# Warm-up matmuls at the head of a Fourier + soft-MoE kernel: six of 512 columns in one pass, or twelve of 64 columns in fp32

## The chip, the cores and the metric

The kernel runs on one core of a Trainium2 chip. A core has TensorE (in the profile PE for matmuls and PEld for weight loads), VectorE (DVE), ScalarE (ACT), GpSimd (POOL) and SyncE (SP, which here only issues DMAs); SPq is SP's instruction queue. The metric is the device time of one execution in microseconds. The profile comes from one further execution; its span runs from the first to the last instruction of the program.

## The reference

The input is `x` with 8 batches of 2496 tokens of 256 features. Each batch goes through a Fourier transform along the tokens, a complex linear layer, a soft threshold and the inverse transform; the result goes through a soft mixture of experts. Cut to what matters:

```python
X = np.fft.rfft(x, axis=1); Xr, Xi = X.real, X.imag
Yr = Xr @ w_r - Xi @ w_i + b_r
Yi = Xr @ w_i + Xi @ w_r + b_i
Yr = np.sign(Yr) * np.maximum(np.abs(Yr) - 0.01, 0.0)     # Yi likewise
y = np.fft.irfft(Yr + 1j * Yi, n=2496, axis=1)             # then, over all tokens:
logits = y @ phi
d = softmax(logits, over tokens); slot_input = d.T @ y      # 32 slots
slot_out = relu(slot_input @ w1[e]) @ w2[e]                 # per expert
out = softmax(logits, over slots) @ slot_out
```

## The kernel before

The transform of 2496 points is done in two stages, 39 x 64. Stage one multiplies the tokens with a table of 39-point Fourier factors (matmuls `pa`, and `q` for batch 0), stage two with 64-point factors (`px`), and the linear layer follows (`pk`, `py`). Later come the inverse stages, the slots, the experts and the output. Every engine runs its instructions in the order in which the code issues them; for most of the kernel a hand-made table of due times, `PLAN`, sets that order.

The head is what matters here. Before anything else GpSimd zeroes a tile `warm` of 128 x 128, and TensorE multiplies it with itself into a PSUM tile `wps` that nobody reads. These are the warm-up dummies:

```python
warm = wtile([128, 128], F32R, "k1", "warm")
P.memset(warm.bitcast(F32), 0.0)
wps = psum("ps", "wps")
for _ in range(6):
    mm(out=wps, lhsT=warm, rhs=warm.unsqueeze(1).broadcast_to([128, 4, 128]), start=True, stop=True)
```

`F32R` is fp32 in one pass: a matmul is one weight load and one pass of the moving columns. A matmul on plain `F32` operands stands in the trace as two weight loads and two passes. The broadcast makes 512 moving columns out of the 128 of `warm`.

Behind the dummies TensorE does batch 0's first stage as 44 plain fp32 matmuls `q` (a weight load of 128 columns of `x`, 120 moving columns of the Fourier table). They read the tile `xf`, which holds the table and the first tokens and comes by SyncE's first DMA, and ten more tiles of `x` that follow it. `wri`, the linear weights, comes behind those. While `q` runs, ScalarE and VectorE copy its results to `at` and `atr`; when `wri` is there, GpSimd makes `wsum` and a difference in place of `wri`, from which ScalarE and VectorE make the weights' high and low parts (`w_r`, `nws`, `wd`, each with `h` and `l`).

Then, in TensorE's order: transposes of `at` into `pa`, copied to `ap` by ScalarE; `px` of the first half of the features from that `ap`; the second half's transposes, copied to `ap` by VectorE; transposes for the next step; `px` of the second half. From each `px` ScalarE makes `xsm` and `xth`, VectorE `xsm` and the two halves of `xs`. `pk` reads `xs`, first for the first half of the features and then, behind six `py`, for the second.

Of the kernel before, what the change touches and what calls it, by code (L numbers as in the profile page):

```python
# [12 lines left out]
F32 = mybir.dt.float32  # L13
F32R = mybir.dt.float32r
# [174 lines left out]
def fourier_soft_moe_kernel(ctx: ExitStack, tc: tile.TileContext, t: dict, out: bass.AP):  # L189
# [21 lines left out]
    def psum(tag, name):  # L211
        return pp.tile([128, 512], F32, tag=tag, name=name, bufs=psum_bufs[tag])

    def wtile(shape, dt, tag, name):
        if tag == "rte":
            return wqp.tile(list(shape), dt, tag=tag, name=name, bufs=2)
        if tag in a_bufs:
            return wap.tile(list(shape), dt, tag=tag, name=name, bufs=a_bufs[tag])
        if tag in main_bufs:
            return wmp.tile(list(shape), dt, tag=tag, name=name, bufs=main_bufs[tag])  # L220
        return wcp.tile(list(shape), dt, tag=tag, name=name, bufs=chain_bufs[tag])
# [8 lines left out]
    V, A, P = (_InOrder(tc, e) for e in (nc.vector, nc.scalar, nc.gpsimd))  # L230
# [18 lines left out]
    def mm(**kw):  # L249
        tc.keep_in_program_order(nc.tensor.matmul(**kw))  # L250
# [39 lines left out]
        x0.append([xf[:P1, Q1 + e * D : Q1 + e * D + D] for e in range(GP)])  # L290
        pools["f1x"] = xf[:P1, :Q1].rearrange("p (c a r) -> p c a r", c=2, r=R)

    warm = wtile([128, 128], F32R, "k1", "warm")
    P.memset(warm.bitcast(F32), 0.0)
    wps = psum("ps", "wps")
    for _ in range(6):
        mm(out=wps, lhsT=warm, rhs=warm.unsqueeze(1).broadcast_to([128, 4, 128]), start=True, stop=True)

    while len(x0) < G // GP:
        load_x0()  # L300
# [907 lines left out]
    rhs = []  # L1208
# [98 lines left out]
    for j in range(NBLK):  # L1307
# [6 lines left out]
        if not pqs:  # L1314
            pqs = [(k, psum(("pf", "pl")[k % 2], f"pq{k}")) for k in ((0, 1) if j == 0 else (j,))]
            for a in range(2):
                for k, pq in pqs:
                    lo = k * TR - k * TR % F
                    mm(
                        out=pq,  # L1320
                        lhsT=cts[lo][:, k * TR - lo : k * TR - lo + TR],
                        rhs=rhs[a].rearrange("p b d -> p (b d)"),
                        start=(a == 0),
                        stop=(a == 1),
# [4 lines left out]
        if j + 1 == starts[i] + OUTS[i]:  # L1329
            n = OUTS[i] * 512  # L1330
            sp(
                out=out[128 * 512 * starts[i] : 128 * 512 * (j + 1)].rearrange("(p f) -> p f", p=128),
# [68 lines left out]
```

## Time and profile before

| | us |
|---|---|
| time, median of 3 runs | 517.67 |
| the three runs | 517.89, 517.67, 515.95 |
| time of the profiled execution | 516.78 |
| its span | 515.0 |
| busy in the span: TensorE passes, weight loads | 500.7, 440.1 |
| busy in the span: VectorE, ScalarE, GpSimd | 405.7, 312.6, 296.2 |

The time of the profiled execution is 1.78 us more than its span; that lies around the program's instructions. Passes overlap in the records, since the end of a pass is modelled and the next one starts before it.

### The profile page before, as it was taken

How to read it: one execution, taken by the hardware profiler on the slowest of the kernel's cores; microseconds unless marked ns; L12 is line 12 of the kernel's file. 1: busy time of each engine (PE TensorE's matmuls, PEld its weight loads, DVE VectorE, ACT ScalarE, POOL GpSimd, SP SyncE). 2: the span in 40 equal slices, each digit the busy share in tenths (PEclk: the TensorE clock that was granted, in tenths of full speed). 3: DMA queues.
4: the chain of work that ended last, by engine and by line, in shares of the span. 5: the costliest groups of instructions: out<-in, count | busy, mean ns of one | idle time of the engine just before them, and what ended most of it. 6: DMA issues, size and time to landing. Idle time of an engine off the chain costs nothing.

```text
span 515.0 us, 11951 instructions
## 1 busy us (share of the span) xinstructions
PE 500.7 (97%) x4475; PEld 440.1 (85%) x4475; DVE 405.7 (79%) x776; ACT 312.6 (61%) x704; POOL 296.2 (58%) x280
## 2 busy tenths in 40 slices
PE   8999999999999999999999999999999999999992
PEld 7889999999999999998999898889899878468881
DVE  2897787799968898889889988897898866257661
ACT  2776666777676766676667666655534446138761
POOL 0686786768676757675667577867475503153310
PEclk9999999999999999999999999999999999999997
DMA  8655555675665657565656566696685567959998
GB/s 299 229 186 185 182 171 201 177 242 149 257 181 183 165 194 203 175 167 201 188 174 174 211 186 207 163 307 182 242 256 150 199 163 194 410 198 403 408 419 342
DMA packets 87485, 114.91 MB, mean 223 GB/s; under 512 B 46191, under 2 KB 65119, under 8 KB 85891
## 3 DMA queue, kind: packets, MB, share of 16 engines
q1 hardware_dynamic: 86860, 113.65, 66.5%
q8 instruction: 35, 0.57, 0.5%
q10 hardware_dynamic: 567, 0.50, 0.3%
q14 instruction: 23, 0.19, 0.1%
HBM read 66.78 MB, written 47.34 MB: 222 GB/s over the span
## 4 chain that ended last, share of the span: by engine, by line
PE 84%; DMA 6%; DVE 4%; POOL 1%; ACT 1%; issue 1%; SPq 1%; DVEq 0%; ACTq 0%; POOLq 0%
PE py L250 21%; PE px L250 13%; PE pk L250 10%; PE pa L250 10%; PE pq L250 9%; PE pt L634 6%; PE pr L250 3%; PE pe L250 2%; PE pc L1186 2%; PE pL L250 2%; PE pg L250 2%; PE pd L250 1%; PE hps L250 1%; DMA out<-ost 1%; DMA gp<-gd 1%; DMA wri<-in_w 1%
## 5 line engine op out<-in xcount | busy, mean ns | idle before, releaser
L185 POOL TENSOR_TENSOR xs<-xsm,xs 128x256 fp32r<-128x256 f32 x77 | 63.3, 823 | 96.4 <-DVE xs L185 66.3
L185 POOL TENSOR_TENSOR rt<-ut,rt 128x512 f32<-128x512 f32 x79 | 104.7, 1326 | 15.1 <-DVE rt L185 13.8
L185 POOL TENSOR_TENSOR xl<-xr,xh 117x512 fp32r<-117x512 f32 x72 | 97.7, 1357 | 12.9 <-ACT xh L185 12.9
L250 PE MATMUL px<-smov,ap 128*128 128x128 f32 x640 | 85.1, 276 | 0.1
L250 PEld LDWEIGHTS px<-smov,ap 128*128 128x128 f32 x640 | 80.3, 192 | 4.8 <-DVE xsm L185 0.3
L185 DVE SCALAR_TENSOR_TENSOR ut<-py,pk,k 128x256 f32<-128x256 f32 x160 | 69.5, 475 | 11.7 <-PE py L250 11.0
L185 ACT CAST xth<-px 128x512 fp32r<-128x512 f32 x80 | 46.9, 587 | 43.6 <-PE px L250 21.6
L185 ACT COPY ast<-pa 128x512 f32<-128x512 f32 x75 | 44.2, 589 | 46.1 <-PE pa L250 46.1
L185 DVE TENSOR_TENSOR xtl<-px,xth 128x512 fp32r<-128x512 f32 x80 | 54.6, 683 | 18.6 <-ACT xsm L185 18.6
L250 PE MATMUL pk<-xs,w_rh 128*128 128x256 f32 (+1 forms) x320 | 66.1, 290 | 0.1
L185 DVE TENSOR_SCALAR rt<-ut 128x512 f32<-128x512 f32 x69 | 65.5, 949 | 0.6
L250 PE MATMUL py<-xth,nwsh 128*128 128x256 f32 (+1 forms) x160 | 53.2, 333 | 0.1
L250 PEld LDWEIGHTS pk<-xs,w_rh 128*128 128x128 f32 x320 | 51.9, 189 | 0.9 <-DVE xs L185 0.6
L185 ACT CAST xh<-xr 117x512 fp32r<-117x512 f32 x75 | 47.4, 635 | 0.4 <-DMA xr<-in_x 0.4
L634 PE MATMUL pt<-pk,rt 128*128 128x128 f32 x320 | 45.2, 274 | 0.0
L250 PE MATMUL py<-xth,wdh 128*128 128x256 f32 (+1 forms) x160 | 44.8, 280 | 0.0
L250 PE MATMUL py<-xtl,nwsh 128*128 128x256 f32 (+1 forms) x160 | 44.6, 279 | 0.0
L250 PE MATMUL py<-xtl,wdh 128*128 128x256 f32 (+1 forms) x160 | 44.5, 278 | 0.0
L250 PE MATMUL py<-xth,wdl 128*128 128x256 f32 (+1 forms) x160 | 44.5, 278 | 0.0
L250 PE MATMUL py<-xth,nwsl 128*128 128x256 f32 (+1 forms) x160 | 44.4, 278 | 0.0
L250 PE MATMUL pk<-xs,w_rl 128*128 128x256 f32 (+1 forms) x160 | 44.4, 278 | 0.0
L185 ACT COPY T<-pt 128x512 f32<-128x512 f32 x66 | 39.2, 601 | 6.8 <-PE pt L634 5.1
(197 smaller groups left out, 1192.3 us busy)
## 6 DMA issues: line engine op xcount, KB each, us to landing
xr<-in_x SPq DMA_DIRECT2D x35, 512.0 KB
ap<-adr SPq DMA_DIRECT2D x70, 256.0 KB
adr<-ast SPq DMA_DIRECT2D x21, 768.0 KB
out<-ost SPq DMA_DIRECT2D x12, 1024.0 KB
w<-in_moe_w SPq DMA_DIRECT2D x21, 512.0 KB
out<-ost SPq DMA_DIRECT2D x14, 512.0 KB
hl<-in_moe_w SPq DMA_DIRECT2D x6, 512.0 KB
x<-in_x SPq DMA_DIRECT2D x10, 256.0 KB
```

What stands on the lines that cost most here:

```text
L185: return lambda *a, **k: self.tc.keep_in_program_order(f(*a, **k))
L250: tc.keep_in_program_order(nc.tensor.matmul(**kw))
L634: tc.keep_in_program_order(nc.tensor.transpose(out=out, in_=in_, identity=identity))
L1186: nc.tensor.transpose(out=pc[:, i * P1 : (i + 1) * P1], in_=chls[b][x][:, 2 * (r + i) : 2 * (r + i) + 2].rearrange("p g h s -> p (g h s)") ...
```

## The change

The tile `warm` becomes plain fp32, and six dummies of 512 columns become twelve of 64. A plain fp32 matmul is two weight loads and two passes, so that 12 instructions of TensorE (6 and 6) become 48 (24 and 24).

```diff
-    warm = wtile([128, 128], F32R, "k1", "warm")
-    P.memset(warm.bitcast(F32), 0.0)
+    warm = wtile([128, 128], F32, "k1", "warm")
+    P.memset(warm, 0.0)
     wps = psum("ps", "wps")
-    for _ in range(6):
-        mm(out=wps, lhsT=warm, rhs=warm.unsqueeze(1).broadcast_to([128, 4, 128]), start=True, stop=True)
+    for _ in range(12):
+        mm(out=wps[:, :64], lhsT=warm, rhs=warm[:, :64], start=True, stop=True)
```

TensorE's instructions at the start of the program, before (a row is a run of equal matmuls; numbers at the end of a name are buffer numbers, and the weight loads are not listed):

```order
L1397 UNCONDITIONAL_BRANCH
L250 MATMUL wps<-warm 128x512 x6
L250 MATMUL q_0_150<-xf 128x2x20x3 x2
L250 MATMUL q_1_153<-xf 128x2x20x3 x2
L250 MATMUL q_0_150<-xf,x_2_89 128x2x20x3 x2
L250 MATMUL q_1_153<-xf,x_2_89 128x2x20x3 x2
```

and the same place of the changed kernel:

```order
L1397 UNCONDITIONAL_BRANCH
L250 MATMUL wps<-warm 128x64 x12
L250 MATMUL q_0_156<-xf 128x2x20x3 x2
L250 MATMUL q_1_159<-xf 128x2x20x3 x2
L250 MATMUL q_0_156<-xf,x_2_95 128x2x20x3 x2
L250 MATMUL q_1_159<-xf,x_2_95 128x2x20x3 x2
```

Only the row of the dummies differs: no other instruction of TensorE has moved against its neighbours, and on the other engines only buffer numbers differ.

## Rows read from the trace of the kernel before

**Rows 1.** The page: busy time by engine, then the chain's shares by engine
```profile
PE 500.7 (97%) x4475; PEld 440.1 (85%) x4475; DVE 405.7 (79%) x776; ACT 312.6 (61%) x704; POOL 296.2 (58%) x280
...
PE 84%; DMA 6%; DVE 4%; POOL 1%; ACT 1%; issue 1%; SPq 1%; DVEq 0%; ACTq 0%; POOLq 0%
```

**Rows 2.** Chain that ended last, first 30 us: start us, us, what
```profile
2.59 5.32 DMA x<-in_x
...
7.93 5.43 DMA wri<-in_w
...
14.84 1.62 POOL wri L185
...
20.00 0.68 PE py L250 x6
20.68 1.03 PE pk L250 x6
```

**Rows 3.** Timeline of TensorE's passes, 0 to 16 us: start, us, count, [idle before]
```profile
0.99 2.93 PE L250 MATMUL wps<-warm 128*128 128x512 f32 x6 [0.99 <-POOL warm L185]
4.46 1.15 PE L250 MATMUL q<-xf 117*128 117x120 f32 x8 [0.54 <-DMA xf<-in_xf]
```

**Rows 4.** Tile `wps`: durations in ns min/median/max, first and last start in us
```profile
L250 PEld LDWEIGHTS wps<-warm x6: 286/330/334, 1.0 to 2.9; 128*128 128x128 f32 x6
L250 PE MATMUL wps<-warm x6: 628/628/793, 1.0 to 3.3; 128*128 128x512 f32 x6
```

**Rows 5.** Groups by line and form, 24 to 40 us: busy us, mean ns
```profile
L250 PE MATMUL pa<-xl,f1h 117*128 117x512 f32 x7 | 2.8, 395 | 0.0
```

**Rows 6.** Groups of weight loads by line and form, 7.4 to 10 us
```profile
L250 PEld LDWEIGHTS q<-xf,x 117*128 117x128 f32 x25 | 2.9, 192 | 0.0
```

**Rows 7.** Timelines from 6.6 us: passes, then weight loads
```profile
6.63 7.41 PE L250 MATMUL q<-xf,x 117*128 117x120 f32 x64
...
6.63 7.22 PEld L250 LDWEIGHTS q<-xf,x 117*128 117x128 f32 x64 [0.31 <-DMA x<-in_x]
```

**Rows 8.** Timeline 13 to 20.5 us, all engines
```profile
15.20 1.11 PE L250 MATMUL px<-smov,ap 128*128 128x128 f32 x8
...
16.15 0.60 PE L634 MATMUL pa<-pk,at 128*128 128x128 f32 x4
16.16 0.83 DVE L185 SCALAR_TENSOR_TENSOR nwsl<-wsum,nwsh 128x512 fp32r<-128x512 f32 x1
...
16.48 0.62 ACT L185 CAST wdh<-wri 128x512 fp32r<-128x512 f32 x1 [0.35 <-POOL wri L185]
...
16.92 0.68 DVE L185 COPY ap<-pa 128x512 f32<-128x512 f32 x1
...
17.65 0.97 PEld L250 LDWEIGHTS px<-smov,ap 128*128 128x128 f32 x8 [0.27 <-DVE ap L185]
...
18.85 0.37 ACT L185 COPY xsm<-px 128x256 f32<-128x256 f32 x1 [0.79 <-PE px L250]
19.12 0.59 ACT L185 CAST xth<-px 128x512 fp32r<-128x512 f32 x1
...
19.76 0.41 DVE L185 TENSOR_TENSOR xsm<-px,xsm 128x256 f32<-128x256 f32 x1
...
20.20 0.29 DVE L185 CAST xs<-xsm 128x256 fp32r<-128x256 f32 x1
```

**Rows 9.** DMA queues: packets, MB, share of 16 engines' span
```profile
q8 instruction: 35, 0.57, 0.5%
```

**Rows 10.** Stretches: busy us (count) by engine, PEclk (granted clock), DMA share, GB/s
```profile
3.00:4.00 1.00, 0.92 (x3) 0.20 (x1) 0.00 (x0) 0.00 (x0) 0.00 (x0) 1.00 0.72 206
...
505.00:509.00 4.00, 0.00 (x0) 0.00 (x0) 0.76 (x2) 0.53 (x2) 0.00 (x0) 1.00 1.01 420
...
512.00:515.00 3.00, 0.00 (x0) 0.00 (x0) 0.00 (x0) 0.00 (x0) 0.00 (x0) 0.50 0.17 71
```

## The prediction

> **What bounds the kernel now.** I read the page first. TensorE's passes fill 97% of the span, and the chain of work that ended last lies on TensorE for 84% [rows 1]. So what delays TensorE early, and is not absorbed in the head, is likely to reach the end one to one. The question is what TensorE does with a delay in the head, and for that I followed the chain through the first 30 us [rows 2]: it runs over the transfers of `x` and of `wri` (7.93 to 13.36 us), GpSimd's arithmetic on `wri` (to 16.46), ScalarE and VectorE, and only from about 19 us on over TensorE. The dummies aren't in it. The timeline of TensorE shows why: the dummies run from 0.99 to 3.92 us, TensorE then idles 0.54 us until `xf` has landed, and `q` starts at 4.46 [rows 3]. TensorE is ahead of the chain in the head, by an amount that has to be found.
>
> **What clock the dummies ran at.** The stretches print a granted clock of 1.00 for the first microseconds too, and 0.50 only at the end, after TensorE had done nothing for over 4 us [rows 10]. At the start that column is not to be trusted, because the durations speak against it: a dummy pass of 512 columns takes 628 ns [rows 4], a pass of 512 columns later 395 [rows 5]. A dummy's weight load takes 324 ns on average (330 at the median [rows 4]), one of `q` 192 [rows 6]. The dummies step by (2.93 - 0.63) / 5 = 0.46 us. So the dummies ran at the lower of the two levels, 1.2 GHz, and `q` at 2.4 GHz: the clock rose between the start of the last dummy (3.3 us) and that of `q` (4.46).
>
> **The change part by part.** Out go 6 weight loads and 6 passes, which end 0.54 us before they would hold anything up. In come 24 weight loads and 24 passes. That plain fp32 doubles them is seen in `q`: two matmuls into each of two tiles read `xf` in the program, and the trace has x8 [rows 3]. The memset is as before, and no other instruction moves.
>
> A pair of a 128-column fp32 load and a 64-column pass is in no row. The nearest are the pairs of `q`, with 120 columns: 64 of them step by (7.41 - 0.28) / 63 = 0.113 us [rows 7] at the full clock. `px`, with 128 columns, steps by (1.11 - 0.28) / 7 = 0.119 [rows 8], and `py`, with up to 256 columns, by 0.68 / 6 = 0.113 [rows 2]. Columns hardly matter at this size, so the load seems to set the step, and 64 columns should not be quicker than 120: 0.113 us at the full clock. At the lower level a load's row is 330 / 192 = 1.7 times as long, half a clock would make it twice: 0.19 to 0.226 us. I take 0.22, near the doubled step. From below, were the pass the limit, a pair would cost 64/120 of 0.113, or 0.06 us at the full clock and 0.12 at the lower one.
>
> If the clock rises at about 4.0 us, inside the bracket of before, then (4.0 - 0.99) / 0.22 = 13 pairs are done by then, and 11 more take 11 x 0.113 = 1.24 us. The dummies end at 5.25 and `q` starts 0.79 us late. With the rise at 3.3 us the same sum gives 10 pairs and 14 x 0.113, an end at 4.9; with the rise at 4.46, 15 pairs and 9 x 0.113, an end at 5.5. So `q` is 0.4 to 1.0 us late; with the pass as the limit it would not be late at all, since 24 x 0.12 = 2.9 us ends where the old dummies ended.
>
> The Trainium skill, TensorE: Matmul & The Clock Gate, section LDWEIGHTS (loading the stationary operand), gives a load as its columns over 1.2, thus 107 ns for 128 columns. By that 24 loads would take an estimated 2.6 us, end near 3.6 us, and delay nothing. The trace has 192 ns for the same load of `q` at the full clock and 330 for the dummies', so I go by the trace.
>
> **What absorbs the delay.** Two slacks stand in TensorE's way. First, the weight loads of `q` stop 0.31 us at 6.63 us for a tile of `x` [rows 7]. A late TensorE finds that tile there, and 0.79 becomes 0.48. From then on TensorE runs without a stop to `px` at 15.20, so 0.48 us arrives at the transposes of 16.15. They end at 16.75 [rows 8]. VectorE copies them to `ap` only from 16.92 on, because it is at `nwsl` from 16.16 to 16.99 [rows 8]; so 0.17 us more is absorbed. What is left, 0.31 us, delays the second `px`, which waits at 17.65 for VectorE's `ap` [rows 8]. From there it is a relay without slack: ScalarE waits 0.79 us for that `px` and makes `xsm` and `xth` (18.85 to 19.71), VectorE follows at 19.76 and 20.20 to 20.49 [rows 8], and the second `pk` starts behind six `py` at 20.68 [rows 2]. `px` of the first half ends at 16.31, and ScalarE, busy with the weights to 17.10 [rows 8], has 0.79 us of slack there; nothing of that path moves.
>
> So the end moves by the lateness of `q` less 0.48 us: 0.79 - 0.48 = 0.3 us, with 0 to 0.5 from the bounds. Against the profiled execution that is 516.78 + 0.3 = 517.1. The median of before lies 0.89 us above that execution, so the forecast is **517.67 + 0.3 = 518.0 us**, a change of 0.06%. The three runs of before differ by 1.94 us or 0.37%: under about 0.5% (2.6 us) a measurement of this kernel can hardly be told from no change.
>
> **The rivals.** *The dummies do not raise the clock* (slower). Short passes and long loads are not what raised it before: there passes filled 0.92 us of the microsecond before 4 us and loads 0.20 [rows 10]. If the clock stays low, 24 pairs end at 0.99 + 24 x 0.22 = 6.3 us, `q` is 1.8 us late, and runs at the lower level itself until the clock rises. The old dummies ran 2.3 to 3.5 us before it did; if `q` runs as long at the lower level, it loses half of that, 1.2 to 1.7 us. Together 3.0 to 3.5 less 0.48: 2.5 to 3.0 us, or 520.2 to 520.7. It decides the sign by 2.6 us when `q` has lost 3.1 us in all. Against it: `q` itself, whose pairs are also loads with short passes, kept the clock. But keeping is not raising, and no row shows a rise from such work. If the clock stays low longer, each further microsecond of `q` costs half of one.
>
> *The dummies end before `xf` lands* (no change at all): a short pass makes the pair short, 0.12 us or less, or the clock rises sooner. Then the time is 517.7. The Trainium skill's figure for a load, on the page named above, would lead here too. For it speaks that nothing in the rows has 64 columns; against it, that 120, 128 and 256 columns step alike.
>
> *Code loading*: the 36 extra instructions shift all of TensorE's program against the blocks in which its code is fetched. The instruction queue moved 35 packets, 0.57 MB in all [rows 9], or 16 KB each, and 0.5% of 16 engines' 515 us is 41 us, or 1.2 us a packet. Should one more block be waited for, the price is 1.2 us, 518.9; a shift may also take away such a wait. I found no stop of TensorE that the waits lay on such a packet, so this is small.
>
> *Faster by a more even start*: TensorE no longer idles 0.54 us before `q`, which could steady the clock in runs where it now rises late. In the profiled run `q` was at full pace from its first instructions, so there is nothing to win there; that one run of three was 1.9 us quicker leaves it possible, at about 516.
>
> **How the numbers follow.** The forecast (0 to 0.5 us late) has 0.50, dummies that end in time 0.20, a clock that stays low 0.17, code loading 0.06, the even start 0.07. The first two and code loading are within 0.5%, as is the mild end of the third (520.2 is +0.49%) and most of the even start (516 is -0.3%); medians that scatter add a little to both sides. That makes faster by over 0.5% 0.05, within 0.5% 0.79, slower by over 0.5% 0.16. For 8 in 10 the range reaches from 516.1, where the even start and the quick runs lie, to 520.6, nearly the top of the low-clock case.
>
> **What would show it.** In the changed kernel's timeline there should be 24 loads and 24 passes of `wps` from 0.99 us, stepping by about 0.22 us and later 0.113, with their end near 5.2; no idle time for `xf`; little or none for `x` near 6.6; loads of `q` of 192 ns from the first one; and the second `px` some 0.3 us after 17.65. Loads of `q` near 330 ns would show the low clock, and passes of `q` that still wait at 4.46 for `xf` the second rival. The prediction is wrong if the stages past 21 us change by more than the head hands them.

## The result and the profile after

The changed kernel takes 519.77 us (median of 11 runs, 518.75 to 521.34), the kernel before 517.41 in the same comparison (11 runs, 515.16 to 518.87). The ratio is 1.0058, with a 95% interval from 1.0045 to 1.007: slower by 0.6%, or 2.3 to 3.6 us; the medians alone differ by 2.4 us. The range held the time only because it had been drawn nearly to the top of the first rival. The likeliest case, 518.0, did not come, and the first rival did.

The page of the changed kernel, busy time by engine and the chain's shares:

```profile
PE 503.7 (97%) x4493; PEld 444.4 (86%) x4493; DVE 404.7 (78%) x776; ACT 312.7 (60%) x704; POOL 296.0 (57%) x280
...
PE 91%; DVE 3%; DMA 3%; ACT 1%; issue 1%; SPq 0%; DVEq 0%; POOL 0%; ACTq 0%; POOLq 0%
```

18 passes and 18 loads more than in [rows 1], 36 instructions in all, and TensorE's share of the chain goes from 84% to 91%. The chain's first 30 us say why:

```profile
0.99 5.38 PE wps L250 x24
6.38 10.34 PE q L250 x80
...
20.30 1.08 PE px L250 x8
21.38 0.02 issue
21.40 0.37 ACT xsm L185
21.77 0.50 ACT xth L185
...
23.11 1.17 PE pk L250 x6
```

In [rows 2] the chain ran over the transfers and over the arithmetic on `wri`. Now it lies on TensorE from the first dummy on: the dummies and `q` have become the bound of the head. The weight loads of the timeline, the first row of the passes of `q`, and the tile `wps` (ns min/median/max):

```profile
0.99 5.20 PEld L250 LDWEIGHTS wps<-warm 128*128 128x128 f32 x24 [0.99 <-POOL warm L185]
6.07 1.83 PEld L250 LDWEIGHTS q<-xf 117*128 117x128 f32 x8
```

```profile
6.17 2.01 PE L250 MATMUL q<-xf 117*128 117x120 f32 x8
```

```profile
L250 PEld LDWEIGHTS wps<-warm x24: 288/333/338, 1.0 to 5.9; 128*128 128x128 f32 x24
```

The loads step by (6.07 - 0.99) / 24 = 0.212 us, all at the length of the low clock, and `q` starts at 6.17 where it started at 4.46 [rows 3], without any wait for `xf`. Then the loads of `q`, between 6.4 and 9 us and between 9.4 and 12 us (busy us, mean ns):

```profile
L250 PEld LDWEIGHTS q<-xf 117*128 117x128 f32 x8 | 1.8, 333 | 0.0
L250 PEld LDWEIGHTS q<-xf,x 117*128 117x128 f32 x6 | 1.4, 330 | 0.0
```

```profile
L250 PEld LDWEIGHTS q<-xf,x 117*128 117x128 f32 x25 | 2.9, 192 | 0.0
```

Up to 9 us `q` runs at the lower level (1.2 GHz), afterwards at 2.4 GHz with the 192 ns of [rows 6]. The stretches of 1 us show the same without durations, by the passes that touch each of them. Their clock column again reads 1.00 throughout, and so cannot be used here:

```profile
8.00:9.00 1.00, 1.00 (x6) 1.00 (x6) 0.00 (x0) 0.00 (x0) 0.00 (x0) 1.00 1.02 381
9.00:10.00 1.00, 1.00 (x11) 1.00 (x10) 0.66 (x2) 0.48 (x2) 0.00 (x0) 1.00 1.06 406
```

The relay behind `q`, in the timeline:

```profile
17.88 1.11 PE L250 MATMUL px<-smov,ap 128*128 128x128 f32 x8
...
20.20 0.97 PEld L250 LDWEIGHTS px<-smov,ap 128*128 128x128 f32 x8
...
21.40 0.37 ACT L185 COPY xsm<-px 128x256 f32<-128x256 f32 x1 [1.12 <-PE px L250]
```

Against [rows 8] the first `px` is 2.68 us late, the second 2.55 and ScalarE's `xsm` 2.55. In [rows 8] the second `px` had waited 0.27 us for VectorE; that wait is gone. The span ends 2.6 us later (517.6 against 515.0). In these two profiles, then, what the head hands over at 21 us is what the end shows; how far that holds in others is said below.

### The profile page after: what moved, and what is told of

It is laid out like the page before. It is cut to its first block, busy times and chain, and to the rows that moved or that the text cites. A ratio compares the mean times of both kernels' runs of the same rounds, so it can differ in the third digit from the quotient of the medians.

```text
span 517.6 us, 11987 instructions
## 1 busy us (share of the span) xinstructions
PE 503.7 (97%) x4493; PEld 444.4 (86%) x4493; DVE 404.7 (78%) x776; ACT 312.7 (60%) x704; POOL 296.0 (57%) x280
## 4 chain that ended last, share of the span: by engine, by line
PE 91%; DVE 3%; DMA 3%; ACT 1%; issue 1%; SPq 0%; DVEq 0%; POOL 0%; ACTq 0%; POOLq 0%
PE py L250 21%; PE px L250 13%; PE pq L250 10%; PE pa L250 10%; PE pk L250 9%; PE pt L634 7%; PE pr L250 4%; PE q L250 2%; PE pc L1186 2%; PE pe L250 2%; PE pL L250 2%; DMA gp<-gd 2%; PE pg L250 2%; PE pd L250 1%; PE hps L250 1%; PE po L250 1%
```

## The experiments

Three theories stood against each other. **Clock**: the short passes leave the clock low, and `q` pays for that on top of the dummies' length. **Lateness**: the dummies are only too long. **Code**: 36 more instructions shift TensorE's program against the blocks in which it is fetched. Every experiment edits the dummies and nothing else. How late a thing is counts from the first profile of the kernel before. Differences in microseconds are the ratio less 1, times the median of before in the same comparison (517.16 us for the first four, 516.89 for the next two).

**Full columns.** The changed kernel with 128 columns in place of 64.

```diff
-        mm(out=wps[:, :64], lhsT=warm, rhs=warm[:, :64], start=True, stop=True)
+        mm(out=wps[:, :128], lhsT=warm, rhs=warm, start=True, stop=True)
```

> Twelve plain fp32 dummies as in the change, but of 128 columns: the same 24 loads and 24 passes at the same step of 0.2135 us while the clock is low, and the same number of instructions. Clock theory (short passes leave the clock low, and q pays for it): the clock rises near 4.2 us as before, 15 pairs are done by then and 9 more at 0.113, q starts near 5.2 at full pace, 0.75 late, of which 0.48 is absorbed: +0.3 us on the kernel before. Code theory (36 instructions more shift TensorE's code): as the change, +2.4 to +3.0 us. If the columns don't matter to the clock: as the change too, with q's first loads at 333 ns.

Measured: ratio 1.0014 (1.0002 to 1.0026), +0.7 us. Instructions and data type are those of the change, and by the ratios some three quarters of the loss is gone. Its timeline of passes and its loads of `q` between 6.9 and 7.6 us:

```profile
0.99 5.12 PE L250 MATMUL wps<-warm 128*128 128x128 f32 x24 [0.99 <-POOL warm L185]
5.95 1.05 PE L250 MATMUL q<-xf 117*128 117x120 f32 x8
```

```profile
L250 PEld LDWEIGHTS q<-xf,x 117*128 117x128 f32 x8 | 1.0, 192 | 0.0
```

`q` starts 0.22 us before that of the changed kernel, and at the full clock: eight passes take 1.05 us and not 2.01. So the clock rose during these dummies, though later than I took it to (`q` at 5.95, expected near 5.2). Its second `px`:

```profile
18.53 0.97 PEld L250 LDWEIGHTS px<-smov,ap 128*128 128x128 f32 x8
```

It is 0.88 us late where that of the change is 2.55. The code theory falls with this run, and so does lateness as the only cause: `q` is nearly as late at its start, and by the ratios a quarter of the time is lost. A second profile was taken:

> The kernel with twelve fp32 dummies of 128 columns again, for a second profile. Clock theory: the clock rises during the dummies here too, and q's first loads take 192 ns. If they take 333 ns, the columns do not decide and the first profile was luck.

In it `q` starts at 6.20 and again takes 1.05 us for its first eight passes:

```profile
6.20 1.05 PE L250 MATMUL q<-xf 117*128 117x120 f32 x8
```

But here the clock rose only as the dummies ended. Their loads (ns min/median/max) are all long; the last takes 327 ns, the first of `q` 225 and the next 192:

```profile
L250 PEld LDWEIGHTS wps<-warm x24: 286/333/333, 1.0 to 5.8; 128*128 128x128 f32 x24
```

**Half as many.** The changed kernel with six of its twelve dummies.

```diff
-    for _ in range(12):
+    for _ in range(6):
         mm(out=wps[:, :64], lhsT=warm, rhs=warm[:, :64], start=True, stop=True)
```

> Six of the change's twelve dummies: 12 pairs at 0.2135 end near 3.55 us, so nothing is late and q starts at 4.46. Clock theory: q starts at the lower level and stays there some 2.9 us as in the changed kernel, which costs 1.45 us less 0.48 absorbed: +1.0 us on the kernel before. Lateness theory (the dummies are only too long): +0.0. Code theory: 12 instructions more than before instead of 36, +0.0 or a third of the change's +2.4 to +3.0.

Measured: 1.0025 (1.0016 to 1.0034), +1.3 us. Nothing is late here, and a loss remains, though less than half of the change's. The timeline has `q` at 3.96, waiting for `xf`, at the slow pace; the stretches show it slow up to 10 us:

```profile
3.96 2.06 PE L250 MATMUL q<-xf 117*128 117x120 f32 x8 [0.15 <-DMA xf<-in_xf]
```

```profile
9.00:10.00 1.00, 1.00 (x7) 1.00 (x6) 0.00 (x0) 0.00 (x0) 0.00 (x0) 1.00 1.06 406
10.00:11.00 1.00, 1.00 (x11) 1.00 (x11) 0.45 (x1) 0.48 (x2) 0.00 (x0) 1.00 1.05 404
```

**None.** The kernel before without its dummies.

```diff
-    for _ in range(6):
-        mm(out=wps, lhsT=warm, rhs=warm.unsqueeze(1).broadcast_to([128, 4, 128]), start=True, stop=True)
```

> No dummies at all. Clock theory: the change's dummies do nothing for the clock, so none is as good as six of them: q starts at 4.46 at the lower level, +1.0 us on the kernel before and the same as with six short ones. Lateness theory and code theory: +0.0 or less.

Measured: 1.0023 (1.001 to 1.0036), +1.2 us, the same as six short dummies within the intervals. So the short ones show no use. In its profile `q` waits for `xf` and then runs slowly until about 8 us:

```profile
3.92 2.06 PE L250 MATMUL q<-xf 117*128 117x120 f32 x8 [3.92 <-DMA xf<-in_xf]
```

```profile
7.00:8.00 1.00, 1.00 (x8) 1.00 (x6) 0.56 (x2) 0.35 (x2) 0.00 (x0) 1.00 1.04 393
8.00:9.00 1.00, 1.00 (x11) 1.00 (x10) 0.55 (x1) 0.00 (x0) 0.00 (x0) 1.00 1.04 383
```

> The kernel without dummies again, for a second profile: q starts near 3.9 us at loads of 333 ns and stays there until some time between 7 and 11 us; its second px comes 0.5 to 2 us later than 17.65.

The second profile has it slow until 10 us, and its second `px` starts at 19.38 us (in the first profile at 18.51):

```profile
9.00:10.00 1.00, 1.00 (x7) 1.00 (x6) 0.00 (x0) 0.00 (x0) 0.00 (x0) 1.00 1.06 406
10.00:11.00 1.00, 1.00 (x11) 1.00 (x11) 0.61 (x2) 0.48 (x2) 0.00 (x0) 1.00 1.05 406
```

So the time from the start of `q` to the rise differed by about 2 us between these two executions of one kernel.

**Light dummies.** The kernel before with four of its dummies and twenty light ones, so that TensorE has the change's number of instructions.

```diff
-    for _ in range(6):
+    for _ in range(4):
         mm(out=wps, lhsT=warm, rhs=warm.unsqueeze(1).broadcast_to([128, 4, 128]), start=True, stop=True)
+    for _ in range(20):
+        mm(out=wps[:32, :32], lhsT=warm[:, :32], rhs=warm[:, :32], start=True, stop=True)
```

> The change's count of instructions (24 loads, 24 passes), but of another kind: four one-pass dummies of 512 columns as before (to about 2.7 us), then twenty one-pass dummies with a load of 32 columns and 32 moving columns. Those take at most 0.1 us each, so they end between 4.5 and 4.9 us and what they are late is absorbed. Clock theory: +0.0 if the clock rises as before the change, +1.0 to +1.5 if the light ones keep it low, which q's first loads show (192 or 333 ns). Code theory: as the change, +2.4 to +3.0 us, with q at full pace.

Measured: 1.0006 (0.9994 to 1.0018), +0.3 us. The same number of instructions again costs nothing like 2.4 us, which is the second run against the code theory. The clock theory, for the case that the light ones keep the clock low, was met in the profile but not in the time: `q` starts at 3.94 at the slow pace, and the second `px` at 19.04 is 1.4 us late.

```profile
3.94 2.04 PE L250 MATMUL q<-xf 117*128 117x120 f32 x8
```

> The kernel with four long and twenty light dummies again, for a second profile. Its time (+0.3 us) was less than its profile's head showed (second px 1.4 us later than in the first profile of before, q at the low level from 3.94 to about 9 us). If the time of the rise differs from one execution to the next, this profile may show q at the low level for less long; if the light dummies always keep the clock low until about 9 us, the same picture comes back and the small time stays unexplained.

The second profile has the same picture: `q` slow until 10 us and the second `px` at 19.49. The two profiled executions were slow in time as well: the first, with 518.74 us, is one of the two slowest of the twelve runs (516.32 to 518.81, median 517.68), and the second took 518.38 where the kernel before took 516.29 in that comparison. So the profiles may show only the slower executions of this kernel. Whether the clock rose sooner in its faster ones, no profile shows, and why its ratio gives only 0.3 us stays open.

**Sixteen long ones.** Lateness with the work that raised the clock before: the kernel before with 16 dummies in place of 6.

```diff
-    for _ in range(6):
+    for _ in range(16):
         mm(out=wps, lhsT=warm, rhs=warm.unsqueeze(1).broadcast_to([128, 4, 128]), start=True, stop=True)
```

> Sixteen one-pass dummies of 512 columns: late like the change's, but with the work that raised the clock before. Clock theory: the clock rises near 4.2 us (at most 5.6, as with the dummies of 128 columns), 7.5 dummies are done by then at 0.427, the other 8.5 take 1.8 us at 0.2155; q starts near 6.0, 1.6 to 2.1 us late but at full pace (loads of 192 ns). Less 0.48: +1.1 to +1.6 us on the kernel before. Lateness theory (the change's dummies cost only by their length, to 6.17): as the change, +2.4 to +3.0.

Measured: 1.0047 (1.0033 to 1.006), +2.4 us, more than the clock theory expected. The time is what the lateness theory had named, but it does not speak for it: `q` came 0.7 us later than the changed kernel's, because the clock rose only after 5 us. And it came at full pace:

```profile
6.89 1.05 PE L250 MATMUL q<-xf 117*128 117x120 f32 x8
```

```profile
19.47 0.97 PEld L250 LDWEIGHTS px<-smov,ap 128*128 128x128 f32 x8
```

`q` is 2.43 us late and the second `px` 1.82, so 0.61 is absorbed. Lateness alone can thus cost nearly as much as the change did, but with a later `q`.

> The kernel with sixteen dummies of 512 columns again, for a second profile: the clock rises during the dummies, at a time between 3.3 and 6 us, and q starts between 5.5 and 7.0 us at loads of 192 ns. Its second px comes 1.4 to 2.0 us later than 17.65.

In the second profile `q` starts at 7.41, again with 1.05 us for eight passes, and the second `px` at 19.98: 2.95 late, 2.33 left. Both are past what was expected, since the first load under 200 ns came only at 6.7 us.

**Eight long ones.** Two more than before, to fill the hole ahead of `q`.

```diff
-    for _ in range(6):
+    for _ in range(8):
         mm(out=wps, lhsT=warm, rhs=warm.unsqueeze(1).broadcast_to([128, 4, 128]), start=True, stop=True)
```

> Eight one-pass dummies of 512 columns in place of six, to fill the hole before q: they end at 0.99 + 8 x 0.427 = 4.4 us at the latest, so q is late by 0.5 us at most, which is absorbed. Clock theory: +0.0 us on the kernel before, or -0.3 to -0.5 if the clock rises late in some executions of that kernel and the longer work prevents it. Lateness theory: +0.0.

Measured: 1.0011 (1.0002 to 1.002), +0.6 us. There is nothing to win in the hole; no version tried here beats the kernel before. In its profile the clock had not risen when `q` began: the eight passes take 1.37 us, and three loads of `q` between 4.6 and 5.1 us take 325 ns on average.

```profile
4.57 1.37 PE L250 MATMUL q<-xf 117*128 117x120 f32 x8
```

The slow start of `q` is absorbed, as the first `px` is not late (15.14 us). The second `px` is, by 0.3 us, but it waits for VectorE's `ap`, and VectorE had been 1.60 us at `w_rl`, 0.90 in the kernel before.

**Both kernels again.** Second profiles of the two.

> The kernel before once more, for a second profile of its head: q's first loads at 192 ns, as in the first profile, if the clock has risen by then in every execution; near 333 ns for some us if the rise comes at another time from one execution to the next. xf lands between 3.9 and 4.5 us.

> The changed kernel once more, for a second profile of its head: dummies to 6.17 us at a load of 333 ns, q's first loads at 333 ns for 2 to 5 us. If the clock rose during the dummies here, the theory that they leave it low falls.

Before (`q` of the timeline, then the loads of `q` from 6.4 to 7.4 us), and the changed kernel (the same two):

```profile
3.81 1.31 PE L250 MATMUL q<-xf 117*128 117x120 f32 x8
```

```profile
L250 PEld LDWEIGHTS q<-xf,x 117*128 117x128 f32 x10 | 1.2, 192 | 0.0
```

```profile
6.17 2.01 PE L250 MATMUL q<-xf 117*128 117x120 f32 x8
```

```profile
L250 PEld LDWEIGHTS q<-xf 117*128 117x128 f32 x6 | 1.4, 333 | 0.0
```

In the kernel before `xf` landed earlier this time, and earlier than expected; `q` began at 3.81 while the clock was just rising (1.31 us for eight passes, 1.15 in [rows 3]), and the second `px` started at 16.91. The changed kernel repeats its start to the hundredth, but its stretches show it slow until after 10 us, over a microsecond longer than in its first profile; its second `px` starts at 20.82.

```profile
9.00:10.00 1.00, 1.00 (x7) 1.00 (x6) 0.56 (x1) 0.32 (x2) 0.00 (x0) 1.00 1.05 399
```

**Could the low clock of the change be chance?** The 24 short dummies end 5.1 us after the first one began, and a rise can come later than that: 5.7 us in the second profile of sixteen long ones. So that the clock stayed low to their end would prove little by itself. The time of the rise says more. In the seven profiles whose dummies all have 128 or 512 columns, the first load under 200 ns starts 3.2 to 5.7 us after the first dummy; without dummies it starts 4.0 and 6.3 us after the first `q`. In the changed kernel it starts 8.2 and 9.5 us after the first dummy, with six short ones 9.1. Counted from the first `q` these three are 3.1, 4.4 and 6.1 us, as if the short dummies had not been there. Chance is thus unlikely, though with one or two profiles of each kernel not excluded. That it is the columns is shown for plain fp32 only; 64 columns in one pass were not tried.

## Why the prediction held only at its edge, point by point

**What bounds the kernel: right.** TensorE was ahead of the chain in the head, and a delay that got through it went to the end: 2.55 us at the second `px` and 2.6 us at the end of the span in the first two profiles, 3.9 and 3.9 in the second two. So close an agreement is luck. From the second `px` to the end the fourteen profiles took 496.9 to 498.4 us, so one profile carries a head's difference to the end only within 1.5 us: with 128 columns the second `px` was 0.88 and 1.14 us late, and the spans were 2.0 and 0.6 us longer than the first of before. The prediction's last sign of being wrong, stages past 21 us that change by themselves, can't be read any finer than that.

**The pair of load and pass: right.** 0.22 us was taken at the low clock, 0.212 was measured, and 64 columns step as 120 do: the first 8 loads of `q`, at the low clock, by (1.83 - 0.33) / 7 = 0.214. Since 64, 120 and 128 columns step alike, the load sets the step here. By the figure for a load that the Trainium skill gives (TensorE: Matmul & The Clock Gate, section LDWEIGHTS (loading the stationary operand)), the dummies would have ended at an estimated 3.6 us; they ended past 6. Its 107 ns is near the step of 0.113 us at the full clock, and half of the step here. The rival that they end before `xf` lands is refuted.

**The step that failed: "if the clock rises at about 4.0 us, inside the bracket of before".** The bracket belonged to dummies of 512 columns, and I carried it over to dummies of 64. The clock did not rise during these in either profile; behind twelve of the same with 128 columns it was up as `q` began, in both. Even for 512 columns the bracket was that of one execution: with eight and sixteen of them the first load under 200 ns came at 5.3, 5.8 and 6.7 us. The forecast's 0.79 us of lateness was therefore 1.71, and the loss on `q` itself, taken as nothing, came on top: 14 pairs at about 0.21 us in place of 0.113 are 1.4 us (20 pairs and 2.0 us in the second profile).

**The first rival was the case.** It had put `q` 1.8 us late (1.71 measured) and the loss at the low clock at 1.2 to 1.7 us (1.4 in the first profile, 2.0 in the second), which gave 520.2 to 520.7 and +2.5 to +3.0 us. The medians differ by 2.4 us; the ratio gives 3.0. Its chance of 0.17 was too small, since nothing but the fact that `q` keeps the clock once it is up stood against it. The row that spoke for it, 0.92 us of passes to 0.20 of loads [rows 10], was weak ground, and that it pointed the right way is luck: in the same microsecond the changed kernel, and then the one with 128 columns, fill it alike, and only the second kind was followed by a rise before `q`.

```profile
3.00:4.00 1.00, 1.00 (x6) 1.00 (x6) 0.00 (x0) 0.00 (x0) 0.00 (x0) 1.00 1.06 390
3.00:4.00 1.00, 1.00 (x7) 1.00 (x6) 0.00 (x0) 0.00 (x0) 0.00 (x0) 1.00 1.05 405
```

**The slacks: right in place, a little off in size.** 0.48 us was predicted to be absorbed. Of the change's 1.71 + 1.4 = 3.1 us, 2.55 is left, so 0.56; with 128 columns 1.49 became 0.88 (0.61), with sixteen long ones 2.43 became 1.82 (0.61). The first slack was larger than the 0.31 us that the loads stood idle: the load before that stop starts at 6.13 us, so at its step of 0.113 the next was due at 6.24 and came 0.39 late, at 6.63. The first eight passes behind the wait for `xf` took 0.1 us more than where nothing is waited for (1.15 to 1.05). The second slack was 0.12 and not 0.17: with 128 columns the first `px` is 1.00 us late, the second 0.88.

**Code loading: refuted as a cause.** Two kernels with 24 loads and 24 passes of dummies lie at +0.7 and +0.3 us, the first with the change's instructions and other operands only. **The even start: not seen.** Eight long dummies fill the hole and are no faster.

How much of the loss is lateness and how much the low clock is settled only roughly. The low clock alone, with nothing late, costs 1.2 to 1.3 us (no dummies, six short ones); lateness at the full clock costs 0.7 us with `q` at 5.95 and 2.4 us with `q` at 6.89 (first profiles). The change has both. Its single runs spread over 2.6 us. The rise, 1.3 us later in one of its two profiles than in the other, and the 1.5 us by which the part past the head varies could make that up, but it was not tested.

## What to carry to other kernels

A warm-up dummy is there for the clock, so judge it by what the first real instructions show: the length of their weight loads (192 or 333 ns here) tells the level even where the granted clock column does not. A time at which the clock rose belongs to the work that raised it; with other work it is an assumption, and the case in which it does not rise has to be priced and given its weight. Dummies that do not raise the clock win nothing, and where they end after the first data have landed they are worse than none, since they stand in the queue ahead of the first real matmul: twelve short ones cost 3.0 us, six 1.3 and none at all 1.2.

## What the runs showed of the hardware

Two kinds of dummies with equal loads, equal steps at the low clock (0.21 us) and equal numbers differed only in their moving columns, 64 and 128. With 128 the clock was up by the second load of `q`, in two of two profiles; with 64 the first load under 200 ns came 3.1 and 4.4 us after the first `q`. Behind short, light or no dummies, real work of the same kind, `q` with 120 columns, was followed by the rise in all seven profiles, between about 3 us (the changed kernel's first profile) and 6 us (six short dummies; none, second profile) after it began. And the granted clock column read 1.00 in stretches in which loads took 333 ns.
